# Another order of VectorE's and TensorE's work in a decode block: attention values, second queries and an early product

## The chip, the cores and the metric

One Trainium2 chip, of which the kernel uses one core. The metric is the device time of one execution in microseconds (us). The matrix engine is TensorE (PE in the profile; PEld is its weight load), the vector engine VectorE (DVE), the scalar engine ScalarE (ACT), GpSimd is POOL, and SP is the engine that issues almost all transfers here.

## The reference, cut to what matters

One token (a row `x` of 640 values, bf16) passes a transformer block in decoding: layer norm, attention over a cache of 4096 keys and values in 32 heads of 128, a residual, layer norm, a gated feed-forward part of width 1728 with tanh-GELU, a residual.

```python
q = (layernorm(x) @ wq).reshape(32, 128)
scores = einsum("hd,hkd->hk", q, k_cache) * 128 ** -0.5
o = einsum("hk,hkd->hd", softmax(scores), v_cache)
h = x + o.reshape(4096) @ wo
g, u = layernorm(h) @ w_gate, layernorm(h) @ w_up
out = h + (gelu(g) * u) @ w_down
```

The two caches are 33.6 MB each; with the weights the kernel reads 84.23 MB from HBM.

## The kernel before, in words

The 32 heads are worked in four groups of eight, g = 0 to 3. A group's keys (8.4 MB) lie in one buffer of 128 partitions: 16 partitions per head, 256 keys of 128 values on each. There are three such buffers, shared by keys, values and weights in turn (`kb` and `vb`, lines 135 and 136), so a load can be issued only when the buffer's last user is done.

`query(g)` (L290) makes the queries of groups g and g + 1: 20 matmuls of TensorE into four PSUM tiles (`pq`), and then, on VectorE, a "pick" of each partition's own head: two masked copies (L306) and a sum (L311) per group, followed by a copy on ScalarE to `qb`. It is called for g = 0 and g = 2.

`scores(g)` (L345 on) goes through the group's keys in eight pieces s. For each, VectorE multiplies 128x4096 keys in place by the query (`mult`, the "product", L322); TensorE folds the products with eight matmuls by the identity into a PSUM tile (`fold`, L334 for the first, which loads the weights, and L285 for the seven others); VectorE sums the rest (`red`, L341) into `sc`. There are two PSUM tiles, so a fold waits for the reduce two pieces back. VectorE's order is product (g,0), product (g,1), reduce (g,0), product (g,2), reduce (g,1), and so on, reduce (g,7). `kfree[g]` is the end of fold (g,7).

`soft(g)` (L354 on): on VectorE the maximum (L356), a small transpose and two small steps (L357 to L360), on ScalarE the exponential with its sum (L363), then on VectorE `P`, the weights spread over the eight heads (L366). After that VectorE masks the sums (`rsm`, L370), TensorE adds them over the partitions (L372, into `pm`), and VectorE inverts them (`rz`, L374).

`values(g)` (L376): 64 matmuls of TensorE with `P` and the values (L379). `vfree[g]` is their end. `outs(g)` (L385): on VectorE a masked copy (L387) and a sum (L390), a small product of TensorE (`po`, L393), and on VectorE the product with `rz` (L395).

Every engine works through its own list strictly in the order in which the Python program emits it; `Sched` (L43) adds a wait where an instruction needs another engine's result, and leaves it out where that engine's list has already waited for it. VectorE's and TensorE's order is thus the order of the calls at L398 to L421. SP's list holds the loads in this order: wq, keys 0, values 0, then each after a wait: keys 1 (after the matmuls of query(2)), values 1 (kfree[0]), keys 2 (vfree[0]), keys 3 (kfree[1]), values 2 (vfree[1]), values 3 (kfree[2]), wo and w_gate (kfree[3]), w_up and w_down (vfree[2]; a last piece of w_down waits for a memset of GpSimd), and the output.

After the four groups come the product with wo (L465), the layer norm (L250), gate and up products (L483), GELU on VectorE (L503 to L512, which ends in `hm`) and the product with w_down (L518), the cast (L522) and the output's transfer.

Of the kernel before, what the change touches and what calls it, by code (L numbers as in the profile page):

```python
# [7 lines left out]
ALU = mybir.AluOpType  # L8
# [14 lines left out]
HG = 8  # L23
NG = H // HG
# [83 lines left out]
def bass_sequential_preLN__gqa_block_cached__glu_gated_geglu__decode_kernel(  # L108
# [14 lines left out]
    def sb(name, shape, dt):  # L123
        return nc.alloc_sbuf_tensor(name, shape, dt)
# [20 lines left out]
    rs = sb("rs", [128, NG], FP32)  # L145
    rsm = sb("rsm", [128, HG], FP32)
# [5 lines left out]
    rz = sb("rz", [128, H], FP32)  # L152
# [5 lines left out]
    hmask = sb("hmask", [128, HG], FP32)  # L158
# [37 lines left out]
    pz = pm  # L196
    pd = pf[0]

    def vec(fn, waits=()):
        return S.op("vector", fn, waits)  # L200
# [29 lines left out]
    def cache(src, g):  # L230
        return src[0, g * HG:(g + 1) * HG, :, :].rearrange("h (q r) d -> (h q) (r d)", r=R)

    def load_k(g, wait):
        d_k[g] = S.dma("sync", "k%d" % g, lambda s: s.dma_start(
            kb[g][:, :, :].rearrange("p r d -> p (r d)"), cache(A_k_cache, g)), [wait])

    def load_v(g, wait):
        d_v[g] = S.dma("sync", "v%d" % g, lambda s: s.dma_start(
            vb[g][:, :, :].rearrange("p r d -> p (r d)"), cache(A_v_cache, g)), [wait])
# [38 lines left out]
    def again(t, out, lhsT, rhs, stop, col=None, start=False):  # L278
        m = mybir.InstMatmult(
            name=nc.get_next_instruction_name(), engine=mybir.EngineType.PE,  # L280
            ins=[t.lower_ap(rhs), t.lower_ap(lhsT, for_matmul_weights=True)], outs=[t.lower_ap(out)],
            start_tensor_calc=start, stop_tensor_calc=stop,
            tile_size=(128, 128 if col is None else 32), tile_position=(0, col or 0), ldweights=False,
            bass_skip_group_check=col is not None)
        return t.add_instruction(m)  # L285
# [4 lines left out]
    def query(g):  # L290
        tok = None
        for c in range(NC_D):
            for i in range(4):
                n0 = g * HG * DH + 512 * i

                def mm(t, c=c, i=i, n0=n0):
                    dst, src, last = pq[i][:, :], wq_sb[:, c, n0:n0 + 512], c == NC_D - 1
                    if i == 0:
                        return t.matmul(dst, xb[:, c, :], src, start=(c == 0), stop=last)  # L299
                    return again(t, dst, xb[:, c, :], src, last, start=(c == 0))  # L300
                tok = S.op("tensor", mm, [t_xb, d_wq, t_qt[0]], token=(c == NC_D - 1 and i == 3))
        for i in range(4):
            half, gg = i % 2, g + i // 2
            lo, hi = half * 64, half * 64 + 64
            h0 = half * HG // 2
            a = t_qt[0] = vec(lambda v, i=i, lo=lo, hi=hi, h0=h0: v.tensor_tensor(  # L306
                out=xm[lo:hi, :, :], in0=pq[i][lo:hi, :].rearrange("p (h d) -> p h d", d=DH),
                in1=hmask[lo:hi, h0:h0 + 4].unsqueeze(2).to_broadcast([64, 4, DH]), op=ALU.mult),
                [tok, t_hmask, t_qf[0]])
            if half:  # L310
                t_qf[0] = vec(lambda v: v.reduce_sum(  # L311
                    xz[:, :], xm[:, :, :].rearrange("p h d -> p d h"), axis=AX.X),
                    [a, t_qb[gg - 1] if gg else None])
                t_qb[gg] = S.op("scalar", lambda a, gg=gg: a.copy(qb[:, gg, :], xz[:, :]), [t_qf[0]])
        return tok

    fold_done, red_done = {}, {}
    t_p, t_pv, t_acc, t_rz, t_z = ([None] * NG for _ in range(5))
    t_ext, t_ex = None, None

    def mult(g, s):
        return vec(lambda v: v.tensor_tensor(  # L322
            out=kb[g][:, s * RP:(s + 1) * RP, :], in0=kb[g][:, s * RP:(s + 1) * RP, :],
            in1=qb[:, g, :].unsqueeze(1).to_broadcast([128, RP, DH]), op=ALU.mult),
            [d_k[g], t_qb[g]])
# [13 lines left out]
    def red(g, s):  # L339
        n = g * NP + s  # L340
        red_done[n] = vec(lambda v: v.reduce_sum(  # L341
            sc[:, s * RP:(s + 1) * RP],
            pf[n % 2][:, :].rearrange("p (r w) -> p r w", r=RP), axis=AX.X), [fold_done[n], t_ex])

    def scores(g):  # L345
        t_mul = mult(g, 0)
        for s in range(NP):
            fold(g, s, t_mul)
            if s + 1 < NP:
                t_mul = mult(g, s + 1)  # L350
            red(g, s)
        kfree[g] = fold_done[g * NP + NP - 1]

    def soft(g):  # L354
        nonlocal t_ex
        a = vec(lambda v: v.reduce_max(mx[:, g:g + 1], sc[:, :], axis=AX.X), [red_done[g * NP + NP - 1]])  # L356
        a = vec(lambda v: v.transpose(mt[:, :], mx[:, g:g + 1].to_broadcast([128, 32])), [a])  # L357
        a = vec(lambda v: v.reduce_max(
            mh[:, :], mt[:, :].rearrange("p (t i) -> p t i", t=2), axis=AX.X), [a])
        a = vec(lambda v: v.scalar_tensor_tensor(  # L360
            out=mj[:, :], in0=mh[:, :], scalar=-SCALE, in1=tmask[:, :], op0=ALU.mult, op1=ALU.mult,
            accum_out=nb[:, g:g + 1]), [a, t_tmask])
        t_ex = S.op("scalar", lambda a: a.activation(  # L363
            ex[:, :], sc[:, :], ACTF.Exp, bias=nb[:, g:g + 1], scale=SCALE,
            accum_out=rs[:, g:g + 1]), [a, t_p[g - 1] if g else None])
        t_p[g] = vec(lambda v: v.tensor_tensor(  # L366
            out=P[:, :, :], in0=ex[:, :].unsqueeze(2).to_broadcast([128, R, HG]),
            in1=hmask_bf[:, :].unsqueeze(1).to_broadcast([128, R, HG]), op=ALU.mult),
            [t_ex, t_hbf, t_pv[g - 1] if g else None])
        a = vec(lambda v: v.tensor_scalar(  # L370
            rsm[:, :], hmask[:, :], rs[:, g:g + 1], 0.0, ALU.mult, ALU.add), [t_z[g - 1] if g else None])
        t_z[g] = S.op("tensor", lambda t: t.matmul(  # L372
            pz[:, 8:8 + HG], ones[:, :], rsm[:, :], start=True, stop=True), [a, t_rz[g - 1] if g else None])
        t_rz[g] = vec(lambda v: v.reciprocal(rz[:, g * HG:(g + 1) * HG], pz[:, 8:8 + HG]), [t_z[g]])  # L374

    def values(g):  # L376
        for i in range(NV):
            r, q = i * VR, 32 * (i % 4)
            t_pv[g] = S.op("tensor", lambda t, i=i, r=r, q=q: t.matmul(  # L379
                pv[g % 2][q:q + 32, :], P[:, r:r + VR, :], vb[g][:, r:r + VR, :],  # L380
                start=(i < 4), stop=(i >= NV - 4)),
                [t_p[g], d_v[g], t_qt[0], t_ext], token=(i == NV - 1))
        vfree[g] = t_pv[g]

    def outs(g):  # L385
        nonlocal t_ext
        a = vec(lambda v: v.tensor_tensor(  # L387
            out=xm[:, :, :], in0=pv[g % 2][:, :].rearrange("p (r d) -> p r d", r=VR),
            in1=rmask[:, :].unsqueeze(2).to_broadcast([128, VR, DH]), op=ALU.mult), [t_pv[g], t_rmask, t_ext, t_qf[0]])
        t_ext = vec(lambda v: v.reduce_sum(  # L390
            xz[:, :], xm[:, :, :].rearrange("p r d -> p d r"), axis=AX.X),
            [a, t_acc[g - 1] if g else t_qb[NG - 1]])
        t_acc[g] = S.op("tensor", lambda t: t.matmul(  # L393
            po[:, g * HG:(g + 1) * HG], xz[:, :], hsel[:, :], start=True, stop=True), [t_ext, t_hsel])
        return vec(lambda v: v.tensor_mul(  # L395
            aT[:, g * HG:(g + 1) * HG], po[:, g * HG:(g + 1) * HG], rz[:, g * HG:(g + 1) * HG]), [t_acc[g], t_rz[g]])

    for g in range(0, NG, 2):  # L398
        t_qlast = query(g)
    load_k(1, t_qlast)  # L400
    scores(0)
    load_v(1, kfree[0])
    soft(0)
    values(0)
    load_k(2, vfree[0])
    outs(0)
    scores(1)
    load_k(3, kfree[1])
    soft(1)
    values(1)  # L410
    load_v(2, vfree[1])
    outs(1)
    scores(2)
    load_v(3, kfree[2])
    soft(2)
    scores(3)
    values(2)
    outs(2)
    soft(3)
    values(3)  # L420
    t_aT = outs(3)  # L421

# [13 lines left out]
    for i in range(len(WD_CUTS) - 1):  # L436
        lo, hi = WD_CUTS[i], WD_CUTS[i + 1]
        tok = S.dma("sync", "wd%d" % i, lambda s, lo=lo, hi=hi: s.dma_start(
            wd_sb[:, lo:hi, :],
            B_w_down[0:MF, :].rearrange("(p b) n -> p b n", b=NM)[:, lo:hi, :]), [vfree[2]])  # L440
# [116 lines left out]
```

## Time and profile before

| | us |
|---|---|
| time, median of 3 runs | 206.66 (205.73 to 207.01) |
| profiled execution: its own time | 207.06 |
| profiled execution: its span | 205.81 |
| VectorE busy | 130.1 (63%) |
| TensorE busy (weight loads beside it) | 117.2 (57%) |
| DMA queue 1, share of 16 engines | 95.5% |
| mean granted TensorE clock | 0.85 |

The span is the time from the first to the last instruction; the execution's own time holds what lies around it too. Busy shares are means over the whole span; the clock is the share of full speed that TensorE was granted. The rows of slices cut the span in 40 equal parts of 5.1 us, each digit being tenths. A piece of the chain of waits is a start, a duration, the engine, what it writes and the line. In the table of stretches each row is start:end, length, and then for each engine its busy time and (xcount) of instructions: PE, PEld, DVE, ACT, POOL; after those the granted clock, the DMA share and GB/s. The DMA share of a short stretch counts a packet where it begins, so it can be over 1.

### The profile page before, as it was taken

How to read it: one execution, taken by the hardware profiler on the slowest of the kernel's cores; microseconds unless marked ns; L12 is line 12 of the kernel's file. 1: busy time of each engine (PE TensorE's matmuls, PEld its weight loads, DVE VectorE, ACT ScalarE, POOL GpSimd, SP SyncE). 2: the span in 40 equal slices, each digit the busy share in tenths (PEclk: the TensorE clock that was granted, in tenths of full speed). 3: DMA queues.
4: the chain of work that ended last, by engine and by line, in shares of the span. 5: the costliest groups of instructions: out<-in, count | busy, mean ns of one | idle time of the engine just before them, and what ended most of it. 6: DMA issues, size and time to landing. Idle time of an engine off the chain costs nothing.

```text
span 205.8 us, 1609 instructions
## 1 busy us (share of the span) xinstructions
PE 117.2 (57%) x826; PEld 24.6 (12%) x552; DVE 130.1 (63%) x162; ACT 6.0 (3%) x18; POOL 1.1 (1%) x6
## 2 busy tenths in 40 slices
PE   1008474196662747676446476670586686195783
PEld 1000000000000310000022000000000012133643
DVE  5100445979995257999652979977889973704132
ACT  3000000000001000000000000001000000100000
POOL 0000000000000000000000000000000001000000
PEclk9999969669998596999958889999589999757555
DMA  7999999999999999999999999999999989999960
GB/s 247 462 502 408 420 408 408 420 535 459 396 420 420 408 411 420 522 446 408 433 408 424 408 446 522 408 420 420 420 420 408 459 357 361 430 412 430 403 279 4
DMA packets 2400, 84.32 MB, mean 410 GB/s; under 512 B 281, under 2 KB 474, under 8 KB 858
## 3 DMA queue, kind: packets, MB, share of 16 engines
q1 hardware_dynamic: 2392, 84.23, 95.5%
q8 instruction: 5, 0.08, 0.2%
q14 instruction: 1, 0.01, 0.0%
q10 hardware_dynamic: 2, 0.00, 0.0%
HBM read 84.23 MB, written 0.00 MB: 409 GB/s over the span
## 4 chain that ended last, share of the span: by engine, by line
DVE 55%; PE 33%; DMA 8%; issue 2%; ACT 2%; DVEq 0%
DVE big L322 30%; PE pq L379 10%; PE pf L285 9%; DVE sc L341 8%; DMA wq_sb<-in_A_wq_dram 8%; PE pq L285 5%; DVE P L366 4%; PE pf L465 2%; DVE xm L306 2%; DVE xz L390 2%; PE pf L334 2%; PE pq L299 2%; DVE xz L311 1%; DVE xm L387 1%; ACT ex L363 1%
## 5 line engine op out<-in xcount | busy, mean ns | idle before, releaser
L322 DVE TENSOR_TENSOR big<-big,qb 128x4096 bf16<-128x4096 bf16 x32 | 72.7, 2281 | 0.0
L285 PE MATMUL pf<-big,Ibf 128*128 128x512 bf16 x224 | 60.0, 413 | 0.0
L334 PE MATMUL pf<-big,Ibf 128*128 128x512 bf16 x32 | 13.9, 434 | 36.6 <-DVE big L322 36.6
L341 DVE TENSOR_REDUCE sc<-pf 128x32 f32<-128x512 f32 x32 | 22.0, 686 | 11.1 <-PE pf L285 11.1
L379 PE MATMUL pq<-big,P 128*32 128x512 bf16 x256 | 20.4, 489 | 0.0
L306 DVE TENSOR_TENSOR xm<-pq,hmask 64x512 f32<-64x512 f32 x8 | 5.5, 688 | 22.3 <-PE pq L285 22.1
L387 DVE TENSOR_TENSOR xm<-pq,rmask 128x512 f32<-128x512 f32 x4 | 2.8, 692 | 18.8 <-PE pq L379 18.8
L334 PEld LDWEIGHTS pf<-big,Ibf 128*128 128x128 bf16 x32 | 3.3, 103 | 95.0 <-DVE big L322 95.0
L299 PE MATMUL pq<-wq_sb,xb 128*128 128x512 bf16 x10 | 5.0, 502 | 16.0 <-DMA wq_sb<-in_A_wq_dram 12.0
L372 PE MATMUL pm<-rsm,ones 128*128 128x8 f32 x8 | 2.3, 358 | 19.4 <-DVE rsm L370 19.4
L285 PE MATMUL pq<-wq_sb,xb 128*128 128x512 bf16 x30 | 11.2, 494 | 0.0
L366 DVE TENSOR_TENSOR P<-ex,hmask_bf 128x2048 bf16<-128x2048 bf16 x4 | 9.2, 2293 | 2.7 <-ACT ex L363 2.7
L379 PEld LDWEIGHTS pq<-big,P 128*32 128x32 bf16 x256 | 7.7, 120 | 12.4 <-issue 9.3
L363 ACT ACTIVATE ex<-sc,nb 128x256 bf16<-128x256 f32 x4 | 2.0, 507 | 135.7 <-DVE mj L360 135.7
L393 PE MATMUL po<-hsel,xz 128*128 128x8 f32 x8 | 1.6, 266 | 7.4 <-DVE xz L390 7.4
L372 PEld LDWEIGHTS pm<-rsm,ones 128*128 128x128 f32 x8 | 1.9, 292 | 24.9 <-DVE rsm L370 24.9
L465 PE MATMUL pf<-wo_sb,aP 128*1 128x160 bf16 x128 | 4.4, 338 | 0.1
L299 PEld LDWEIGHTS pq<-wq_sb,xb 128*128 128x128 bf16 x10 | 1.2, 119 | 26.6 <-issue 21.4
L311 DVE TENSOR_REDUCE xz<-xm 128x128 f32<-128x512 f32 x4 | 4.1, 1022 | 0.1
L390 DVE TENSOR_REDUCE xz<-xm 128x128 f32<-128x512 f32 x4 | 4.1, 1018 | 0.1
L465 PEld LDWEIGHTS pf<-wo_sb,aP 128*1 128x1 bf16 x128 | 4.1, 124 | 0.3 <-DVE aP L455 0.3
L468 DVE STREAM_TRANSPOSE th<-pf 128x160 f32<-128x160 f32 x1 | 0.3, 350 | 4.5 <-PE pf L465 4.5
(76 smaller groups left out, 39.8 us busy)
## 6 DMA issues: line engine op xcount, KB each, us to landing
wq_sb<-in_A_wq_dram SPq DMA_DIRECT2D x1, 5120.0 KB, 15.4
wo_sb<-in_A_wo_dram SPq DMA_DIRECT2D x1, 5120.0 KB, 17.2
wg_sb<-in_B_w_gate_dram SPq DMA_DIRECT2D x1, 2160.0 KB, 21.9
wu_sb<-in_B_w_up_dram SPq DMA_DIRECT2D x1, 2160.0 KB, 23.8
wd_sb<-in_B_w_down_dram SPq DMA_DIRECT2D x1, 800.0 KB, 24.6
wd_sb<-in_B_w_down_dram SPq DMA_DIRECT2D x1, 640.0 KB, 25.6
wd_sb<-in_B_w_down_dram SPq DMA_DIRECT2D x1, 480.0 KB, 26.2
wd_sb<-in_B_w_down_dram SPq DMA_DIRECT2D x1, 160.0 KB, 26.1
```

What stands on the lines that cost most here:

```text
L285: return t.add_instruction(m)
L299: return t.matmul(dst, xb[:, c, :], src, start=(c == 0), stop=last)
L306: a = t_qt[0] = vec(lambda v, i=i, lo=lo, hi=hi, h0=h0: v.tensor_tensor(out=xm[lo:hi, :, :], in0=pq[i][lo:hi, :].rearrange("p (h d) -> p h ...
L311: t_qf[0] = vec(lambda v: v.reduce_sum(xz[:, :], xm[:, :, :].rearrange("p h d -> p d h"), axis=AX.X), [a, t_qb[gg - 1] if gg else None])
L322: return vec(lambda v: v.tensor_tensor(out=kb[g][:, s * RP:(s + 1) * RP, :], in0=kb[g][:, s * RP:(s + 1) * RP, :], in1=qb[:, g, :].unsquee ...
L334: return t.matmul(dst, Ibf[:, :], src, start=True, stop=False)
L341: red_done[n] = vec(lambda v: v.reduce_sum(sc[:, s * RP:(s + 1) * RP], pf[n % 2][:, :].rearrange("p (r w) -> p r w", r=RP), axis=AX.X), [f ...
L366: t_p[g] = vec(lambda v: v.tensor_tensor(out=P[:, :, :], in0=ex[:, :].unsqueeze(2).to_broadcast([128, R, HG]), in1=hmask_bf[:, :].unsqueez ...
L379: t_pv[g] = S.op("tensor", lambda t, i=i, r=r, q=q: t.matmul(pv[g % 2][q:q + 32, :], P[:, r:r + VR, :], vb[g][:, r:r + VR, :], start=(i < ...
L387: a = vec(lambda v: v.tensor_tensor(out=xm[:, :, :], in0=pv[g % 2][:, :].rearrange("p (r d) -> p r d", r=VR), in1=rmask[:, :].unsqueeze(2) ...
L390: t_ext = vec(lambda v: v.reduce_sum(xz[:, :], xm[:, :, :].rearrange("p r d -> p d r"), axis=AX.X), [a, t_acc[g - 1] if g else t_qb[NG - 1]])
L465: b = S.op("tensor", lambda t, c=c, j=j: t.matmul(pd[32 * j:32 * j + 1, 0:NQ], aP[:, c:c + 1], wo_sb[:, c, j * NQ:(j + 1) * NQ], start=Fal ...
```

## The change

Four things move, and nothing is added to or taken from what is computed.

- The pick of the second queries (groups 2 and 3) is split off `query` as `pick_q`. It now stands inside scores(0), on VectorE between product (0,2) and reduce (0,1).
- outs(0) stands inside scores(1) and outs(1) inside scores(2), at the same place: after product (g,2), before reduce (g,1); its small product of TensorE stands between fold (g,1) and fold (g,2).
- Product (3,0) stands ahead of reduce (2,7), so ahead of soft(2).
- The mask of the sums and their product of TensorE (`rsm`, L370, and L372) go from `soft` to the head of `values`, the reciprocal (L374) to the head of `outs`; and at the end soft(3) stands ahead of outs(2). In the kernel before the order was scores(3), values(2), outs(2), soft(3), values(3), outs(3).

```diff
-        return tok
+        return tok
+
+    def pick_q(g, tok):
         for i in range(4):
             half, gg = i % 2, g + i // 2
...
-    def scores(g):
-        t_mul = mult(g, 0)
+    early = {}
+
+    def scores(g, between=None, ahead=False):
+        t_mul = early.pop(g, None) or mult(g, 0)
         for s in range(NP):
             fold(g, s, t_mul)
             if s + 1 < NP:
                 t_mul = mult(g, s + 1)
+            elif ahead:
+                early[g + 1] = mult(g + 1, 0)
+            if between and s == 1:
+                between()
             red(g, s)
...
+    def values(g):
         a = vec(lambda v: v.tensor_scalar(
-            rsm[:, :], hmask[:, :], rs[:, g:g + 1], 0.0, ALU.mult, ALU.add), [t_z[g - 1] if g else None])
+            rsm[:, :], hmask[:, :], rs[:, g:g + 1], 0.0, ALU.mult, ALU.add), [t_ex, t_z[g - 1] if g else None])
         t_z[g] = S.op("tensor", lambda t: t.matmul(
             pz[:, 8:8 + HG], ones[:, :], rsm[:, :], start=True, stop=True), [a, t_rz[g - 1] if g else None])
-        t_rz[g] = vec(lambda v: v.reciprocal(rz[:, g * HG:(g + 1) * HG], pz[:, 8:8 + HG]), [t_z[g]])
-
-    def values(g):
...
     def outs(g):
         nonlocal t_ext
+        t_rz[g] = vec(lambda v: v.reciprocal(rz[:, g * HG:(g + 1) * HG], pz[:, 8:8 + HG]), [t_z[g]])
...
-    for g in range(0, NG, 2):
-        t_qlast = query(g)
-    load_k(1, t_qlast)
-    scores(0)
+    t_q = query(0)
+    pick_q(0, t_q)
+    t_q = query(2)
+    load_k(1, t_q)
+    scores(0, lambda: pick_q(2, t_q))
     load_v(1, kfree[0])
     soft(0)
     values(0)
     load_k(2, vfree[0])
-    outs(0)
-    scores(1)
+    scores(1, lambda: outs(0))
     load_k(3, kfree[1])
     soft(1)
     values(1)
     load_v(2, vfree[1])
-    outs(1)
-    scores(2)
+    scores(2, lambda: outs(1), ahead=True)
     load_v(3, kfree[2])
     soft(2)
     scores(3)
     values(2)
+    soft(3)
     outs(2)
-    soft(3)
     values(3)
     t_aT = outs(3)
```

## The prediction

> **What bounds the kernel now.** I read the page's slices first, then the DMA rows, then the chain of waits, then stretches of time.
>
> ```profile
> DVE  5100445979995257999652979977889973704132
> PEclk9999969669998596999958889999589999757555
> DMA  7999999999999999999999999999999989999960
> ```
>
> No compute engine is full, but the DMA row reads 9 from the second slice to the 38th. The queue row gives 95.5% of the 16 engines' span for queue 1. The 84.2 MB are one stream on one queue in program order: wq, K0, V0, K1, V1, K2, K3, V2, V3, wo, wg, wu, wd. The reader should see that no order of compute makes this stream shorter; it can only end its tail sooner, or let the stream run dry. Next, the row of the K2 load, asked for by its line in the stretch 73 to 74.5 us:
>
> ```profile
> L234 SPq DMA_DIRECT2D big<-in_A_k_cache_dram x1: 328/328/328, 73.9 to 73.9; - x1
> ...
> DMA to landing us min/median/max: 39.6/39.6/39.6
> ```
>
> Issued at 73.95, landed 113.59. The same question gives K1 33.28 + 41.5 = 74.80, K0 35.57, K3 132.80, V2 152.15, V3 171.50. K1 and K2 land just before their group's first product (76.34 and 114.03 in the chain): what stands ahead of those two products is already covered by a transfer, to 1.5 and 0.44 us. The chain shows this, and where group 2 and 3 wait:
>
> ```profile
> 111.64 0.70 DVE xm L387
> ...
> 114.03 2.21 DVE big L322
> ...
> 116.75 3.00 PE pf L285 x7
> ...
> 119.77 0.69 DVE sc L341
> ...
> 137.11 1.52 PE pf L285 x7
> ...
> 138.66 0.70 DVE sc L341
> ...
> 143.44 0.15 DVE rsm L370
> ...
> 144.37 2.17 DVE big L322
> ...
> 150.22 0.69 DVE sc L341
> ```
>
> Between products DVE steps by 2.20 (product, L322) + 0.60 (reduce, L341) = 2.80 us. It stops only at a group's first fold, which runs at half clock (3.46 to 3.6 us, against 1.91 at full clock), at its last fold, and for the sum of exponentials (143.44 to 144.37). Stretches on the grid of the clock's changes show when the clock halves:
>
> ```profile
> 99.41:102.82 3.41, 1.39 (x7) 0.00 (x0) 1.71 (x7) 0.14 (x1) 0.00 (x0) 1.00 1.02 442
> 102.82:106.23 3.41, 0.42 (x2) 0.42 (x2) 2.43 (x2) 0.47 (x2) 0.00 (x0) 0.50 0.80 346
> ...
> 171.09:174.50 3.41, 1.56 (x33) 0.55 (x21) 1.71 (x2) 0.00 (x0) 0.63 (x1) 1.00 0.89 372
> 174.50:177.91 3.41, 0.37 (x2) 0.28 (x2) 2.23 (x7) 0.60 (x2) 0.00 (x0) 1.00 0.93 396
> ```
>
> Behind a stretch and its length stands PE's busy time; the third figure from the end is the granted clock. After a stretch with 1.39 us of PE the clock is 0.50; after 1.56 it stays 1.00. It comes back only after a stretch that PE fills (3.41).
>
> **The change, part by part.** Nothing is added or removed; 1609 instructions stand in another order. I write F for the end of the last fold (3,7), 169.06 in the chain.
>
> *Second queries.* DVE's pick for groups 2 and 3 (33.28 to 38.24, 4.96 us) moves from ahead of product (0,0) into scores(0), after product (0,2). Product (0,0) then starts when K0 has landed, 35.57 + 0.1, not 38.24: 2.6 earlier, 5.0 later, so scores(0) ends 2.4 later, at 66.1 instead of 63.71. With the pause on PE one fold there may run cold: from 0 to 3.6 - 2.8 = 0.8 more. P(0) ends 4.08 later (63.71 to 67.79 in the chain), at 70.2 to 71. Product (1,0) behind it waits for K1 at 74.80 in any case: cost nothing, cover 3.8 us; without it, the 2.4 would be paid. The ACT copies of these queries (0.30 each) stand ahead of the exponential that comes 20 us later. On SP, V1's issue waits for kfree[0] and goes from 63.01 to about 65.4, values(0) ends at 76.6, not 73.95, which moves K2's issue; both queue behind transfers that last until about 74 and 93. Cost nothing, covers 8 and 16 us.
>
> *outs(0) into scores(1), outs(1) into scores(2).* For group 1, DVE gains 76.34 - 74.9 = 1.44 at the start and some 1.2 at the first fold (PE has just done values(0), so it is warm), pays 2.60 for outs (2.39 for L387 to L395, 111.64 to 114.03, plus the reciprocal's 0.21). Ends at 101.4 against 101.53. Whatever that is, P(1) ends by 106.4 and K2 lands at 113.59: a cover of 7 us. K3's issue moves by less than 1 us with 12 us of cover. Group 2 is where it counts. Product (2,0): 113.7 for 114.03, -0.33. Its first fold at half clock: the wait before the reduce is 1.25 instead of 1.33, -0.08. outs(1), before in time that K2's transfer covered, now lies on the path: +2.60. While DVE does it, PE pauses from 121.3 to 124.3; the stretch that holds the pause has about 1.4 us of work, like the one at 99.41, so I take fold (2,2) cold: it starts behind the po product at 124.67, ends at 128.3, and its reduce would have been due at 127.65: +0.65 (bounds 0, clock kept, and 1.5, two folds late).
>
> Here a rule is weighed. The row: 1.39 us of work in a stretch did not keep the clock. The Trainium skill, page "TensorE: Matmul & The Clock Gate", section "Why this matters for your kernels", asks for no idle gap over some 3 us between bursts and puts the return to half rate on an idle window; here no window would be idle throughout, so by it this term would be 0 and the sum -0.76. The trace decides for the row.
>
> *Product (3,0) ahead of reduce (2,7).* DVE idles 1.39 us for fold (2,7), 137.27 to 138.66. Product (3,0) fills it: reduce (2,7) comes some 0.8 later, but the 2.20 are done: -1.39. Fold (3,0) runs under soft(2), so its cold wait (148.75 to 150.22, 1.46) goes; next late is fold (3,1), cold as PE then has paused 5 us: 3.6 - 2.8 = +0.83. Together -0.63 (bounds -1.46 and +0.1, if (3,2) is late too). K3 has landed at 132.80, so the early product waits for nothing. V3's issue goes with fold (2,7) from 138.65 to about 141.5, under V2's transfer, which reads until 150: cover 9 us.
>
> *rsm and its product into values, reciprocal into outs.* After P(2), DVE no longer does rsm, waits for pm and inverts: 143.44 to 144.37, -0.93. The wait that rsm gains, on the exponential, costs nothing: P, ahead of it on DVE, has waited for that already. The sum's product of a group waits for the reciprocal of the group before, now in outs; that one is done a whole group earlier. For groups 0 and 1 the order on PE stays.
>
> *The end.* Before, F to the first of values(3) at 179.82: values(2) 3.60, outs(2) 2.39, L356 to the end of P 3.96, rsm 0.19, pm 0.60, in all 10.76 with gaps. After: reduce (3,7) 0.70, rsm 0.17, pm 0.59, values(2) 3.60, P (which waits for values(2), as it overwrites P) 2.31, outs(2) 2.60, rsm 0.19, pm 0.60: 10.76. The first part of soft(3), 1.85, hides under values(2), but values(2) starts 1.45 later and rsm(3) stands behind outs(2). So 0, bounds +-0.6 for the clock in values(3) (6.07 us there, 3.6 at full clock, of which only an edge can move). wu and wd are issued 1.45 later relative to F, behind wo and wg, which transfer until about 191: cover 15 us. POOL's memset ahead of wde moves with them; nothing is behind it.
>
> *The stream's end.* wo is issued when F is reached:
>
> ```profile
> 169.09 0.33 SPq L423 DMA_DIRECT2D wo_sb<-in_A_wo_dram  x1
> ```
>
> and in the stretch from 169.50 to 170.00 no packet begins (0.01); the first of wo begin at 170.05. Most engines have ended V3 at 169.3 to 169.7: the stream stands still for about 0.7 us, in mean. An F 0.7 earlier closes that, a later one widens it. The last wd lands at 201.74, and hm is ready at 201.67: stream and compute tie at the end.
>
> **Sum:** -0.33 - 0.08 + 2.60 + 0.65 - 1.39 - 0.63 - 0.93 + 0 = -0.11 us. The profiled execution took 207.06 for a span of 205.81; the median of the runs shown, 206.66, is 0.40 less. I put the difference on the median: **206.5 us**.
>
> **Rivals.**
> *The clock stays up* (its grid is not tied to the kernel, so the pauses can fall across a border). For it: 1.56 us of work was enough once. Without the cold folds: -0.11 - 0.65 - 0.83 - 1.25 = -2.84. But the stream stops it: with its 0.7 closed the last wd lands at 201.04; last four products 0.5, then 2.03 from the last product to the end as now, 203.6 of span: -2.2, 204.5 us. With one of the three gone, 205.3 to 205.9.
> *The clock stays down longer* (the other side). One mechanism: outs(1) starves PE in scores(2), and each further fold at half clock is 0.8 late, as 3.6 exceeds 2.8. It decides from one more late fold on: one is +0.7, two (fold (2,3) 0.85 and (3,2) 0.7) are -0.11 + 1.55 = +1.44, 208.1 us, and F goes past 170, so the stream waits as well. Against more: a fold stream at half clock fills its stretch, and a full stretch brought the clock back each time.
> *The waits in the chain go as they read there.* Between P and product (1,0), (2,0) there are 8.4 us each; less outs that is 2 x 5.8, about 195 us. The landings of K1 and K2 speak against it; 1 in 100.
>
> **How the numbers follow.** Forecast 0.60 (own range 205.9 to 207.2), clock up 0.20 (204.5 to 205.9), clock down 0.17 (207.2 to 208.1), the rest 0.03, of which 0.01 is the chain's reading and 0.02 a stream that runs dry by over 2 us. A measurement here tells about 1% from no change: 204.6 and 208.7. Faster: a sixth of "clock up", which only at its floor gets there, and the 0.01: 0.04. Slower: a tenth of "clock down", with the runs' own spread (205.73 to 207.01), and the 0.02: 0.04. Same: 0.92. The range 205.1 to 207.7 leaves out four tenths of each clock case and the rest, 0.18.
>
> **What would show it.** Right: products (1,0) and (2,0) start within 0.2 of the landings of K1 and K2; outs(1) takes 2.6 us of DVE between products (2,2) and (2,3); no DVE idle before reduce (2,7); P(3) ends after values(2) and values(3) starts 10.8 after F; F between 168 and 170; the DMA row still full. Wrong: a wait of DVE for a K landing later than here, F beyond 170.5, more than two late folds per group, or values(3) at another clock.

## The result and the profile after

| | before | changed |
|---|---|---|
| median of six executions | 205.87 (205.38 to 207.01) | 203.80 (202.97 to 205.24) |
| profiled execution, its own time and span | 207.06, 205.81 | 202.97, 201.72 |
| F, end of fold (3,7) | 169.06 | 166.41 |
| last piece of w_down landed | 201.74 | 199.30 |

The ratio is 0.989, interval 0.985 to 0.994. The forecast of 206.5 with a range from 205.1 was too slow; the kernel became about 2 us faster. A later measurement of the changed kernel gave 203.69 against 205.52 (0.991, 0.988 to 0.994). The two profiled executions are further apart (4.1 us) than the medians (2.1): the one of before was among its slowest, the one of the changed kernel its fastest. Ratios leave out executions that the measurement counts as disturbed, the medians do not, so the two can differ where a kernel's executions fall into two groups.

The slices of the changed kernel:

```profile
DVE  5100530889898737899962598999889973804231
PEclk9999969679589958859985999999958999969855
DMA  7999999999999999999999999999999999999992
```

The stream is as full as before and ends sooner. The row of K2's load, issued at 78.07, and the chain from there to the end:

```profile
L234 SPq DMA_DIRECT2D big<-in_A_k_cache_dram x1: 328/328/328, 78.1 to 78.1; - x1
...
DMA to landing us min/median/max: 35.2/35.2/35.2
```

```profile
78.07 35.22 DMA big<-in_A_k_cache_dram
113.28 0.02 issue
113.31 4.49 DVE big L324 x2
117.80 0.60 DVE sc L343
118.40 2.20 DVE big L324
120.60 0.12 DVE rz L394
...
122.81 0.17 DVE aT L403
...
144.46 2.21 DVE big L324
...
147.32 3.00 PE pf L285 x7
...
171.32 22.80 DMA wu_sb<-in_B_w_up_dram
```

K2 was asked for 4 us later than before and landed 0.3 us earlier, at 113.28: what stood in the queue in front of it was the same. Product (2,0) starts 0.03 us after the landing. Behind its two products (4.49) the reduce follows at once; before there were 1.33 us of waiting for a fold at half clock. outs(1) takes DVE from 120.60 to 122.98. After P(2) product (3,1) follows directly (144.46), as (3,0) is done. In the chain before there was no transfer after the first; here the chain ends on one, w_up, which lands at 194.12 and for which TensorE waits 1.9 us. In this execution the kernel ends where its stream ends.

At wo, the stretch in which no packet began before (0.01) is filled:

```profile
169.00:169.50 0.50, 0.50 (x16) 0.26 (x12) 0.00 (x0) 0.00 (x0) 0.00 (x0) 1.00 0.76 328
169.50:170.00 0.50, 0.50 (x16) 0.21 (x8) 0.00 (x0) 0.00 (x0) 0.00 (x0) 1.00 1.53 655
```

### The profile page after: what moved, and what is told of

The parts are those of the page before. It is cut to its first block, busy times and chain, and to the rows that moved or that the text cites. A ratio compares the mean times of both kernels' runs of the same rounds, so it can differ in the third digit from the quotient of the medians.

```text
span 201.7 us, 1610 instructions
## 1 busy us (share of the span) xinstructions
PE 117.6 (58%) x826; PEld 22.0 (11%) x552; DVE 129.9 (64%) x162; ACT 6.0 (3%) x18; POOL 1.1 (1%) x6
## 4 chain that ended last, share of the span: by engine, by line
DMA 46%; DVE 36%; PE 15%; issue 1%; ACT 1%; SPq 0%; DVEq 0%
DMA big<-in_A_k_cache_dram 34%; DVE big L324 23%; DMA wu_sb<-in_B_w_up_dram 11%; PE pf L285 6%; DVE sc L343 6%; PE pq L386 5%; DVE P L374 2%; PE pf L336 1%; DVE xm L309 1%; PE pq L490 1%; PE pf L525 1%; DVE xz L314 1%; ACT ex L371 1%; DVE xz L398 1%; PE pm L382 0%
## 5 line engine op out<-in xcount | busy, mean ns | idle before, releaser
L285 PE MATMUL pf<-big,Ibf 128*128 128x512 bf16 x224 | 63.0, 428 | 0.0
L336 PE MATMUL pf<-big,Ibf 128*128 128x512 bf16 x32 | 14.3, 446 | 34.2 <-DVE big L324 34.2
L299 PE MATMUL pq<-wq_sb,xb 128*128 128x512 bf16 x10 | 4.8, 475 | 15.6 <-DMA wq_sb<-in_A_wq_dram 11.6
L374 DVE TENSOR_TENSOR P<-ex,hmask_bf 128x2048 bf16<-128x2048 bf16 x4 | 9.2, 2292 | 5.1 <-PE pq L386 3.1
L285 PE MATMUL pq<-wq_sb,xb 128*128 128x512 bf16 x30 | 10.7, 476 | 0.0
L490 PE MATMUL pq<-wu_sb,hln 128*1 128x416 bf16 x20 | 2.2, 566 | 1.9 <-DMA wu_sb<-in_B_w_up_dram 1.9
L401 PEld LDWEIGHTS po<-hsel,xz 128*128 128x128 f32 x8 | 1.4, 218 | 16.5 <-DVE xz L398 16.5
L490 PE MATMUL pq<-wg_sb,hln 128*1 128x416 bf16 x20 | 2.2, 562 | 1.2 <-DVE hln L264 1.2
```

The costliest lines, as they stand in the source:

```text
L336: return t.matmul(dst, Ibf[:, :], src, start=True, stop=False)
L374: t_p[g] = vec(lambda v: v.tensor_tensor(out=P[:, :, :], in0=ex[:, :].unsqueeze(2).to_broadcast([128, R, HG]), in1=hmask_bf[:, :].unsqueez ...
L490: b = S.op("tensor", lambda t, c=c, j=j, row=row, lhs=lhs: t.matmul(row[:, :, 0:NM], lhs, w[:, c, QF * j:QF * (j + 1)].rearrange("p (i b) ...
```

## The experiments

Theory A: the time from K2's landing to F counts, and whether wo is issued before the stream has run dry. Rival B: the clock happened to stay full in the executions measured, and the order does little. All kernels have the changed kernel's helper functions; "kernel before" means its order of calls. Times are medians; the kernel before stood at 205.4 to 205.7 in each call. F and all other places are read in one profiled execution of each kernel, which need not be one near the median.

### Taking the parts apart

**e1**, the changed kernel without the early product:

```diff
-    scores(2, lambda: outs(1), ahead=True)
+    scores(2, lambda: outs(1))
```

> The changed kernel with product (3,0) back behind soft(2); all else as changed. Theory A (what counts is the time from the landing of K2 to the end of fold (3,7), called F, and whether wo is issued before the stream has run dry): F comes 1.4 to 2.0 us later than in the changed kernel (166.4 to about 168.2), wo is issued at the brink, time 204.8 to 205.9. Rival B (the gain over the forecast was only the clock, which happened to stay full through scores(2), and the order does little): 203.5 to 204.3.

205.64, ratio 0.999 (0.995 to 1.002); F 168.1. With one instruction's place the gain is gone in the median, so B falls, and A's numbers hold. A's account by F is not shown here: the profiled execution took 203.66, the second fastest of twelve, at that same F, and its last piece of w_down landed at 199.96. No execution near the median was profiled.

**e2**, the kernel before with the early product alone:

```diff
-    scores(2)
+    scores(2, ahead=True)
```

> The kernel before with nothing but product (3,0) moved ahead of reduce (2,7). Theory A: F 1.5 to 2.0 us earlier than 169.06, the stream no longer stops at wo, time 203.8 to 204.6. Rival B: no gain beyond 0.4, 205.5 to 205.9.

203.73, ratio 0.992 (0.989 to 0.995); F 167.2, 1.9 earlier. It is as fast as the whole change: on top of it, the other three parts together bring nothing. The stream was not quite whole here: wo was issued at 167.24, and the last wd landed 28.9 us behind V3, against 27.6 in the changed kernel's first profile.

**e3**, the kernel before with outs(0) and outs(1) inside the scores:

```diff
-    outs(0)
-    scores(1)
+    scores(1, lambda: outs(0))
...
-    outs(1)
-    scores(2)
+    scores(2, lambda: outs(1))
```

> The kernel before with nothing but outs(0) and outs(1) moved inside scores(1) and scores(2). Theory A: product (2,0) cannot start before K2 has landed, so outs(1), which was covered by that load, now costs its 2.4 us, less 0.3 for the start and 0 to 1.3 for the first fold: F 0.8 to 2.1 later, wo later by as much, time 206.5 to 208.5. Rival (the wait for values that the chain showed was worth having): faster than before, 203 to 205.

206.62, ratio 1.006 (1.001 to 1.010); F 171.3, 2.3 later, a little more than I expected. The waits of 8 us for values(0) and values(1) that the chain of before shows were worth nothing: K1 and K2 would have been waited for instead.

**e4**, the changed kernel once more.

> The changed kernel itself once more, for a second profiled execution with another place of the clock's grid. Theory A: products (1,0) and (2,0) again start at the landings of K1 and K2, F between 166 and 168, time 203 to 205. Rival B: in an execution with the clock halved during scores(2), F near 168.5 and the time near 205.5, as forecast.

203.69. This profile shows the execution I had forecast: the clock halved in scores(2), twice. Stretches on its grid:

```profile
121.85:125.26 3.41, 1.46 (x8) 0.32 (x3) 2.90 (x6) 0.00 (x0) 0.00 (x0) 1.00 0.80 346
125.26:128.67 3.41, 3.40 (x9) 0.10 (x1) 3.32 (x3) 0.00 (x0) 0.00 (x0) 0.50 1.29 558
```

and of the execution shown above:

```profile
118.23:121.64 3.41, 1.53 (x8) 0.00 (x0) 3.38 (x5) 0.00 (x0) 0.00 (x0) 1.00 1.24 538
121.64:125.06 3.42, 2.13 (x10) 0.32 (x3) 2.94 (x4) 0.00 (x0) 0.00 (x0) 1.00 0.84 364
```

The same pause for outs(1) leaves 1.46 us of PE in one stretch, and the next is at half clock, or 1.53 in another, and the next stays full. F came at 168.8 against 166.4, outside A's range. Yet the execution that was late at F took only 1.0 us more: its span was 202.7, against 205.8 before at nearly the same F (169.06). So F was not all, and B's number for this case (205.5) was missed too: this execution took 204.05.

**e12**, the kernel before with the pick, the sums and soft(3) in their new places:

```diff
-    pick_q(2, t_q)
     load_k(1, t_q)
-    scores(0)
+    scores(0, lambda: pick_q(2, t_q))
...
     scores(3)
     values(2)
-    outs(2)
     soft(3)
+    outs(2)
     values(3)
```

(`rsm`, its product and the reciprocal also as in the changed kernel.)

> The kernel before with the pick of the second queries inside scores(0), the mask and product of the sums in values, the reciprocal in outs, and soft(3) ahead of outs(2); outs(0), outs(1) and product (3,0) where they were. Theory A: the pick costs nothing under K1's load; the sums bring F forward by 0.9, and F to values(3) stays 10.8: 204.5 to 205.6. Rival (these parts make the gain as well): below 204.2; rival (the pick delays the rest): over 206.

206.62, ratio 1.007 (1.003 to 1.011): my expectation failed, and the rival that the pick delays the rest held. The profiled execution was the slowest of twelve (208.55). Its chain reads

```profile
80.99 0.17 DVE aT L403
81.16 2.21 DVE big L324
```

With outs(0) still ahead of product (1,0), the pick's delay (scores(0) ends 3.7 us later than before) goes through values(0), here 1.1 us longer, and outs(0), and the product starts at 81.16 instead of 76.34; product (2,0) at 119.56, F at 173.4. The cover by K1 that I gave the pick exists only where outs(0) no longer stands in between. e13 and e14 take this apart.

**e13**, the pick and outs inside, all else as before, and **e14**, sums and soft(3) alone (their diffs are those above).

> The kernel before with the pick inside scores(0) and outs(0), outs(1) inside scores(1), scores(2); sums, soft(3) and product (3,0) where they were. Theory (the pick's 2.4 us are free only where outs(0) no longer stands between P(0) and product (1,0)): products (1,0) and (2,0) at the landings of K1 and K2, F 169.9 to 171.4, time 205.8 to 207.0, as e3 and not slower than e12. Rival (the pick costs 2.4 wherever it stands inside scores(0)): F 172 or later, 207.5 to 209.

In the profile, products (1,0) and (2,0) stand at the landings and F at 169.3: the pick costs nothing there. My ranges for F and for the time were both missed: 207.4 median, above the 206.6 of e12, with executions from 204.6 to 210.4, ratio 1.004 (1.000 to 1.008). The profiled execution took 205.03, so the mechanism is seen in one of the quickest alone; why others took longer stays open, and the rival (207.5 to 209) is not excluded for them.

> e12 without its pick: only the mask and product of the sums in values, the reciprocal in outs, soft(3) ahead of outs(2). Theory: F 0.9 earlier than in the kernel before, 168.0 to 168.6, and wo with it, F to values(3) 10.8 as before: 204.3 to 205.3. Rival (these parts are what made e12 slow): 206 to 207.

204.25, ratio 0.994 (0.991 to 0.997); F 168.2, 0.9 earlier, as worked out. These parts are not what made e12 slow. The median lies just under my range. Alone they bring 1.4 us, so the early product is not the only part that gains; in e1 they stand beside the pick and outs, which alone costs 1.1 us (e3), and the gain is gone.

### What the end hangs on

**e5**, the kernel before with wo waiting for the five pieces of K3 that it overwrites:

```diff
-        wo_sb[:, :, :], A_wo[:, :].rearrange("(p c) n -> p c n", c=QD)), [kfree[3]])
+        wo_sb[:, :, :], A_wo[:, :].rearrange("(p c) n -> p c n", c=QD)), [fold_done[3 * NP + 4]])
```

> The kernel before, with the load of wo waiting for fold (3,4) and not for fold (3,7): it overwrites only the five pieces of K3 that are folded by then. No engine's work moves; only the stop of the stream at 169.7 to 170.1 goes. Theory A (stream and compute both set the end of the kernel before): the last wd lands 1.5 to 2.4 earlier than 201.74, but hm stays at 201.7, so the time gains 0 to 0.5: 205.4 to 205.9. Rival C (the stop of the stream alone was the price, and the gain of the change is that it closed it): 203.6 to 204.3.

The median, 205.75 (ratio 0.991, 0.986 to 0.997), lies in theory A's range but hides two groups: five executions at 202.8 to 203.1, seven at 205.7 to 206.8, nothing between. The last wd landed at 199.25 in the profiled one (201.6 span). Neither theory had this. No execution of the slower group was profiled. If the stream is unbroken there too, something else makes 3 us, and the granted clock differs: 0.88 to 0.90 in the first five, 0.86 to 0.87 in the others. In the profile of e5 (first line) the product with wo took 2.41 us; in that of before (second fence) 4.46:

```profile
188.14 2.41 PE pf L475 x128
```

```profile
189.15 4.46 PE pf L465 x117
```

From F to the end of `hm` e5 needs 29.4 us, before 32.6, with the same instructions. I formed theory A2: the stretch after F has two lengths, by the clock in values(3) and in the product with wo, and the end is the later of compute and stream. The profiles bear out the second half: in 12 of the 17 the execution ended 2.36 to 2.44 us after the last wd had landed; in the five others (before, e3, e8, e11, e13) compute was last, and the end came 3.3 to 4.2 us after `hm`.

**e6**, the changed kernel with wo issued after values(2):

```diff
-        wo_sb[:, :, :], A_wo[:, :].rearrange("(p c) n -> p c n", c=QD)), [kfree[3]])
+        wo_sb[:, :, :], A_wo[:, :].rearrange("(p c) n -> p c n", c=QD)), [vfree[2]])
```

> The changed kernel, with the load of wo waiting for the end of values(2) and not for fold (3,7), 4.9 us later (171.3). Theory A: the stream stands still for 2.3 to 2.6 us and the end moves by at least that, 206.0 to 208.0. Rival (the loads behind wo have slack enough): 203.5 to 204.3.

207.74, ratio 1.010 (1.007 to 1.013). By the packet records the engines stood idle for 4.5 us in mean (wo issued at 173.2), and the last wd came 5.5 us later after V3 than in an unbroken stream. A break costs more than its idle time.

**e7**, the changed kernel with outs(1) back ahead of scores(2), and **e8**, the changed kernel with wo early as in e5.

```diff
-    scores(2, lambda: outs(1), ahead=True)
+    outs(1)
+    scores(2, ahead=True)
```

> The changed kernel with outs(1) back ahead of scores(2), in the time that K2's transfer covers. F comes some 2 us earlier, 164.2 to 165.0. Theory A with the stream as the end of the changed kernel: no gain beyond 0.5, 203.3 to 203.9, with a longer wait of TensorE for w_up. Rival D (compute still sets the end): 201.6 to 202.2.

203.39, ratio 0.990 (0.986 to 0.993); F 165.8, later than I expected. An F earlier than the changed kernel's by 0.6 to 3 gains at most 0.4 in the median. In the profile the stream is the end: `hm` came at 197.5, the last wd at 199.4.

> The changed kernel with wo waiting for fold (3,4) only. Theory A: in the profiled execution of the changed kernel the stream did not stop, so the best executions stay, and those in which F was late gain: median 203.0 to 203.7, a smaller spread. Rival: no difference at all, 203.8 with the same spread.

204.07, ratio 0.990 (0.986 to 0.994), spread 202.8 to 205.9: no gain, and the spread that I expected to shrink did not, so the rival held. In its profile the stream ended at 199.1 and `hm` came at 199.6: there compute was last, with 6.2 us for values(3) and 3.6 for the product with wo, partly at half clock.

**e9**, the kernel before with spare products in TensorE's pauses after F, and **e10**, the same with wo early:

```diff
+    def warm(n):
+        for _ in range(n):
+            S.op("tensor", lambda t: t.matmul(
+                pf[1][:, :], Ibf[:, :], xb[:, 0:4, :], start=True, stop=True),
+                [red_done[NG * NP - 1]], token=False)
...
     values(2)
+    warm(8)
     outs(2)
+    warm(18)
     soft(3)
     values(3)
+    warm(8)
```

> The kernel before with 41 spare products of TensorE (each 128x512, 0.215 us at full clock, into a PSUM tile that nothing reads any more) put into its pauses after F: 8 behind values(2), 18 behind the product of outs(2), 8 behind values(3), 7 around the second layer norm. They add nothing to the result and are meant to hold the clock at full speed up to the product with w_up. Theory A2 (the stretch from F to the end has two lengths, by the clock in values(3) and in the product with wo, which took 6.04 and 4.46 us in the profile of before; the stop of the stream at wo comes on top): hm 3 to 4 us earlier, the stream's end takes over, time 203.8 to 204.8 with no executions above 205.5. Rival (the spread of before comes from the transfers): no change, 205.3 to 205.9 and the same spread.

204.49, ratio 0.998 (0.994 to 1.001), 203.9 to 206.3; the bound of 205.5 was missed by three executions, and the interval holds 1, so this step alone is not clear of the noise. The product with wo ran at full clock, and the chain ended on w_up, which landed at 196.90: wo had been issued at 169.6, and the stream had broken.

> The spare products of e9 and wo's load waiting for fold (3,4) only, on the kernel before. Theory A2: both causes are taken away, so only the faster of the two modes of e5 is left, 202.7 to 203.3, as fast as the changed kernel or faster, though no product, pick or outs stands elsewhere. Rival (the order of the work counts in itself): 204.5 to 205.9.

202.88, ratio 0.987 (0.983 to 0.992), all executions between 202.72 and 203.04. It is the fastest kernel of the study with the smallest spread, and no product, pick or outs has moved in it. Its chain is on the stream up to the last four products:

```profile
176.23 22.81 DMA wd_sb<-in_B_w_down_dram
199.04 0.04 issue
199.08 0.38 PE pf L539 x12
```

The four kernels (before, e5, e9, e10) are a table of two causes: neither removed, 205.4 to 205.7; the break alone, two groups; the clock alone, 204.5 (not clear of the noise); both, 202.9, and in six executions e5's slower group is gone. That the clock made this group is shown by this step, not by a profile of it.

**e11**, the changed kernel with 18 and 8 spare products behind values(2) and values(3) and 7 around the layer norm.

> The changed kernel with 33 such spare products in its pauses after F (18 behind values(2), 8 behind values(3), 7 around the second layer norm). Theory A2: the changed kernel ends on the stream in nearly all executions, so little is left: 202.8 to 203.6, less spread. Rival (compute still sets its end in many executions): below 202.3.

203.99, ratio 0.994 (0.991 to 0.998): not faster than the changed kernel, and both expectations missed. In its profile F was 168.3, and another wait stands in the chain:

```profile
185.44 2.38 PE pf L480 x127
187.82 3.31 issue
191.13 0.23 PE pf L480
```

The last of 128 products waited 3.3 us for nothing that the profile shows. A packet of the instruction queue begins at 188.7, inside the wait, and takes 0.95 us. In e9 such a packet (186.7, 0.97 us) falls into the same product, which runs without a wait; so the cause stays open.

**e15**, e10 with the early product added.

> e10 with product (3,0) ahead of reduce (2,7) as well, F near 167.3. Theory (in e10 the stream's end is the only thing left): no gain, 202.6 to 203.0. Rival (compute still counts): 201.0 to 202.0.

203.05, just above my range, ratio 0.988 (0.985 to 0.991). F at 167.4, two microseconds earlier than in e10, gains nothing. The end of the unbroken stream is the floor, at 202.7 to 203.3 in e10 and e15.

## Why the prediction failed

**Right.** Products (1,0) and (2,0) start 0.03 us behind their loads, so what DVE waited for in the chain before was replaced by the wait for K1 and K2. outs(1) costs DVE 2.38 us there (2.60 worked out; 0.12 of the reciprocal is on the chain). No idle time is left before reduce (2,7), fold (3,1) is the late one (0.87 for 0.83), and values(3) starts 10.4 after F in one profile, 10.6 in the other (10.76). By parts, F moves with the early product by -1.9 (forecast -2.0), with the sums by -0.9 (-0.93) and with outs by +2.3 (+2.84 from the four terms). With pick and outs together it moved by +0.3 only (e13): there the first fold of scores(2) ran at full clock, in e3 at half. So the pick costs nothing where outs has moved too, and the price of outs depends on the clock.

**The clock term, +0.65 and the cold first fold.** I took one place of the clock's grid for the case. The execution profiled first met the other, with the first fold at 1.9 us and no late fold: F 166.4. e4 met the one forecast, and its F, 168.8 against my 168.95, is in part luck. Fold (2,2) began at full clock and came 0.15 us late, not 0.65:

```profile
124.99 0.23 PE pf L336
125.22 2.83 PE pf L285 x7
128.05 0.02 issue
128.07 0.69 DVE sc L343
```

(The product before this reduce ended at about 127.9.) In its place the first fold cost 1.5 us instead of 1.25, and K2 landed at 113.9, not at the 113.6 that I had carried over. Over the changed kernel's order, F was 166.4, 168.8, 168.3, 168.0 and 168.3 (e6, e8 and e11 have its order up to there), against 169.0 to 169.6 in before, e5, e9 and e10. That is about -1.3 in mean, where I had -0.11.

**The steps behind F.** These two are what failed above all, as they failed even where F came as forecast: in e4 the last wd landed at 200.3 and `hm` came at 198.3, where before both came at 201.7, and the execution took 204.05, not 206.5.

*"The end", 0 with bounds of 0.6.* I carried the 32.6 us from F to `hm` over from one execution, in which the product with wo ran at half clock (4.46 us; 2.4 in e4). In e5, with the same order of the engines' work, it is 29.4, and in e4 29.5. So "stream and compute tie at the end" described one execution: with the product with wo at 2.4 us the stream was last, but for the wait in e11; with it at 3.3 to 4.5 it was compute in before, e3, e8 and e13, and the stream in e2 and e6.

*"The stream's end".* I closed the break by its 0.7 us and put the last landing at 201.04, so the floor at 204.5. The last wd landed 30.2 us behind V3 before, and 27.6 to 27.8 behind it wherever the stream did not break (changed, e5, e7, e8, e10, e15): the break cost 2.6. Idle engines make 0.7 of it; wo's packets took 12.9 us per engine in mean instead of 12.2, another 0.7; the rest lies in the engine that was last, and is not explained. Issues of wo at 167.2 to 168.8 (e1, e2, e4, e11, e14) lost 0.9 to 1.5; at 169.1 to 169.6 (before, e9, e13) 2.0 to 2.9; at 171.3 to 173.4 (e3, e6, e12) 3.3 to 5.5. "An F 0.7 earlier closes that" was right in direction, but the price was almost four times as large, and an F 0.7 to 1.0 earlier (e1, e11, e14) still left 0.9 to 1.5 of it.

**The base.** The 206.66 I started from was the median of three; six gave 205.87. The execution profiled before (207.06) was slower than any of these six, and the whole working rests on it.

**Two readings of the profile.** A first fold at half clock took "3.46 to 3.6 us"; that of group 1 took 3.33 (from 78.60). The clock "comes back only after a stretch that PE fills": in e1 it came back after one with 2.75 us of PE (145.34 to 148.75).

Of the rivals, "the clock stays up" was nearest, with its reason half right (F) and its floor wrong. "The waits in the chain go as they read there" is refuted by e3.

The Trainium skill's rule in "TensorE: Matmul & The Clock Gate", section "Why this matters for your kernels" (an idle window of some 3 us halves the rate) does not tell the cases here apart: in e4 TensorE's pause for outs(1) was 1.95 us and half clock followed, in the execution profiled first it was 2.62 us and the clock stayed.

## What to carry to other kernels

Where a transfer queue is full from start to end, read first when each transfer is issued against when the queue before it drains: a step ahead of a landing is free as long as it ends before that landing (the pick in e13, not in e12), a step behind it may cost time (outs in e3), and the one issue that comes at the brink (here wo) is worth more than the engines' chain shows. Take no stretch at half clock from a single execution as a constant; work out both lengths and ask which of compute and stream ends last in each. Then look for the cheapest way to move the brink: a wait on the part of a buffer that is really needed gave, together with spare products that held the clock (e10), all that four moved parts gave and 0.8 us more.

## What the runs showed of the hardware

- The clock's change hangs on small differences: in e4 1.46 us of PE in a stretch of 3.41 were followed by half clock, in the changed kernel's first profile 1.53 by full clock, and F differed by 2.4 us. PE's busy time alone does not decide: after 1.56 us the clock stayed in before (171.09) and halved in e2 (169.47); after 1.43 (120.20) and 1.47 (79.24) it stayed in e11, after 2.01 (186.13) it halved in e13.
- wo's packets took 12.2 us per engine where wo was issued by 166.4, and 12.6 to 12.9 where it was issued at 167.2 or later, even where the engines hardly stood idle (e11, 12.7, idle under 0.1 us in mean). So a late issue costs more than the idle time that it leaves.
- TensorE once waited 3.3 us before the last of 128 products (e11) for nothing that the profile shows.
